# Clustered attention, feed-forward and soft mixture: narrowing in two slopes through PSUM, 128-column means, own PSUM tiles, low halves on VectorE, a new order

## The chip, the cores and the metric

The kernel runs on one core of one Trainium2 chip. The metric is device time in microseconds of one execution, the median over the timed runs; lower is better. Engines: PE (TensorE), with its weight loads shown apart as PEld, DVE (VectorE), ACT (ScalarE), POOL (GpSimd), SP (SyncE, which here only issues transfers).

## What is computed

Three stages over a batch of 2 with 8 heads, 768 positions and 64 columns a head; all data but w_in and w_out is float32.

```python
# attention, per batch and head; scale = 1/sqrt(64), 16 centroids per head
q_assign = argmax(q_n @ c_n.T); k_assign = argmax(k_n @ c_n.T)   # normalised rows
scores = where(q_assign[:, None] == k_assign[None, :], scale * q @ k.T, -1e9)
x = softmax(scores) @ v                       # -> x: 1536 tokens x 512
# feed-forward, w_in 512 x 2048, w_out 2048 x 512
h = x @ w_in; g = h * clip(h + 3, 0, 6) / 6; x = g @ w_out
# soft mixture: phi 512 x 32 slots, 8 experts of 4 slots, w1 512 x 1024, w2 1024 x 512
logits = x @ phi
slot_in = softmax(logits, over tokens).T @ x
slot_out[e] = relu(slot_in[e] @ w1[e]) @ w2[e]
out = softmax(logits, over slots) @ slot_out
```

w_in and w_out arrive as float64; the chip reads each number as two uint32 words and narrows it to float32.

## The kernel before

**Stages.** Heads 0 to 15 (head i is batch i // 8) go through attention. float32 products are made from float16 pairs (a high half and a low half) so that PE runs at its 16-bit rate. For each head: `cast_hi` and `cast_lo` make the halves of q and k (scaled by SQ = 64), transposed by DMA (head 0: by PE, in `turned`); `as_mm`, `as_max`, `as_put` find the cluster of each row; `cnt_mm` counts empty clusters and makes the mean of v with `wmean` (80 columns); `maxq`, `maxr`, `shift` find the row maxima (L531, L547, L556); then for six key blocks t `scores` (L569, L573), `exps` (L617 and a float16 high half through `high`, L342; or L610 where WHOLE names the block, which then stays float32), `plow` (the low half, by `low`, L352, on POOL) and `pv` (L639 to L660). `finish` divides (L672), `split_x` makes the halves of x.

**Weights.** w_in (8 blocks, `win`) and w_out (8 blocks, `wout`) are narrowed during the first heads by `narrow`: part 0 keeps the sign bits on DVE (L878) and scales the absolute value on ACT into PSUM (L880); part 1 shifts and joins on DVE inside PSUM (L883); part 2 joins the low word on DVE (L888). w_out goes back to DRAM as `wos`; `wphi1` to `wphi3` fold phi into w_out.

**Feed-forward.** 12 token blocks of 128: `hid` (L710), `act` (L727, L729, halves through L342 and L352, then the transpose of g: by DMA, or for the tiles in TURNED by PE into PSUM and copied out by ACT and DVE in turns, L751 and L753), `logits`, `colmax`, `dweights`, `dispatch`. The blocks of batch 0 run among the heads of batch 1; those of batch 1 after the last head.

**Experts.** `zsum` (L1193 on), `slot_in`, `slot_t`, `combine_weights`, `layer1`, `relu`, `turn`, `layer2`, `store2`, and for the last four experts column part by column part (PARTS) `layer2_part` (L1402), `slots_out`, `combine` with the output transfers. Their weights come in chunks (`fetch`, L1019 and L1041) into rooms: ring a (4 rooms, from the start), ring b (9, once attention's memory is given back in `close`), ring c (2, after `close2`), then tiles of earlier stages as they come free.

**Order.** Every function is a generator whose steps end in `yield`. ORDER is a list of event numbers; `flush` runs the next step of the named event, so the list fixes the order of the instructions on every engine and on SP's queue. ROOMS names the buffer of each tile. `keep` events are matmuls without use that keep PE running. Engines run their own queue in order; a step that waits holds what is behind it on its engine.

Of the kernel before, what the change touches and what calls it, by code (L numbers as in the profile page):

```python
# [1477 lines left out]
```

## Time and profile before

| what | us |
|---|---|
| median of 3 timed runs | 479.06 |
| lowest, highest | 476.38, 479.09 |
| span of the profiled execution | 475.5 |

The page gives no time for the profiled execution other than its span; the median of the timed runs is 3.6 us above it.

| engine | busy us | share of the span |
|---|---|---|
| PE | 437.2 | 92% |
| ACT | 316.9 | 67% |
| DVE | 284.3 | 60% |
| POOL | 251.1 | 53% |

Busy time is the time in which an engine had at least one instruction running. PE's matmuls overlap, and their ends are modelled. The share is a mean over stages with different limits, so the rows below are cut by stage.

### The profile page before, as it was taken

The numbers are of one execution on the slowest core, as the hardware profiler recorded it, in microseconds if no ns is written. First come the engines' busy times: TensorE is split into PE (matmuls) and PEld (weight loads), VectorE is DVE, ScalarE is ACT, GpSimd is POOL, SyncE is SP. The second block draws the span as 40 slices with busy tenths as digits, with TensorE's granted clock in tenths as the row PEclk, the third lists the DMA queues.
The fourth block names the chain that finished last, engine by engine and source line by source line (L and its number), as shares of the span: only waits on it lengthen the run. The fifth ranks groups of instructions, "written<-read, shape, count | busy, mean of one in ns | idle before, by whom it ended". The sixth has DMA issues, their size and how long they took to land.

```text
span 475.5 us, 11894 instructions
## 1 busy us (share of the span) xinstructions
PE 437.2 (92%) x4938; PEld 283.1 (60%) x4938; DVE 284.3 (60%) x497; ACT 316.9 (67%) x518; POOL 251.1 (53%) x227
## 2 busy tenths in 40 slices
PE   6779999999979999999999998989998999789973
PEld 5557678777767656656666666754545545442443
DVE  4899999998968387466667759513233223540222
ACT  7369899898965978876789998963545335600121
POOL 5326588785644555666698897984313233130000
PEclk9789999999999999999999999999999999999998
DMA  8777866946794689689473555005996799999998
GB/s 280 187 150 187 193 172 174 271 122 196 244 253 113 177 203 195 139 157 226 112 145 72 54 102 139 3 1 106 314 307 207 158 274 373 406 341 384 339 284 272
DMA packets 133813, 95.50 MB, mean 201 GB/s; under 512 B 96384, under 2 KB 119424, under 8 KB 133760
## 3 DMA queue, kind: packets, MB, share of 16 engines
q1 hardware_dynamic: 129088, 88.95, 71.2%
q10 hardware_dynamic: 4672, 5.80, 3.4%
q8 instruction: 38, 0.62, 0.5%
q14 instruction: 15, 0.12, 0.1%
HBM read 64.06 MB, written 7.34 MB: 150 GB/s over the span
## 4 chain that ended last, share of the span: by engine, by line
PE 66%; DVE 14%; ACT 8%; DMA 6%; issue 3%; POOL 2%; SPq 0%; ACTq 0%; DVEq 0%; POOLq 0%
PE h L710 26%; DVE mxs L547 4%; PE st L569 4%; PE sm L531 4%; PE st L573 4%; PE e L1345 3%; DMA wod<-in_moe_w_out_dram 3%; PE acc L639 2%; PE acc L652 2%; PE z L819 2%; DMA wk<-in_moe_w_dram 2%; ACT p L617 2%; PE acc L645 2%; PE acc L644 2%; PE o L1382 2%
## 5 line engine op out<-in xcount | busy, mean ns | idle before, releaser
L352 POOL TENSOR_TENSOR pp<-p,pp 128x768 f16<-128x768 f32 x72 | 119.7, 1667 | 56.1 <-ACT pp L342 28.0
L710 PE MATMUL h<-wq,xt 128*128 128x512 f16 x576 | 132.1, 379 | 0.0
L547 DVE TENSOR_REDUCE mxs<-sm 128x1 f32<-128x768 f32 x96 | 89.5, 952 | 15.7 <-PE sm L531 15.0
L710 PEld LDWEIGHTS <-xt 128*128 128x128 f16 x576 | 55.2, 98 | 62.0 <-issue 2.5
L352 POOL TENSOR_TENSOR ghl<-r,ghl 128x1024 f16<-128x1024 f32 (+1 forms) x25 | 50.4, 2017 | 61.1 <-ACT ghl L342 55.9
L617 ACT ACTIVATE p<-st 128x768 f32<-128x768 f32 x72 | 57.9, 805 | 15.2 <-PE st L573 13.7
L342 ACT ACTIVATE pp<-p 128x768 f16<-128x768 f32 x72 | 60.3, 842 | 1.4 <-PE acc L652 0.2
L569 PE MATMUL st<-qk1t 128*128 128x384 f16 x192 | 47.6, 329 | 5.5 <-ACT p L617 4.9
L531 PE MATMUL sm<-qk2t 80*128 80x384 f16 x192 | 45.9, 331 | 2.7 <-DVE mxs L547 0.9
L729 DVE SCALAR_TENSOR_TENSOR r<-r,h 128x1024 f32<-128x1024 f32 (+1 forms) x26 | 29.5, 1135 | 31.4 <-ACT r L727 31.3
L573 PE MATMUL st<-qk2t 102*128 102x384 f16 x192 | 47.5, 329 | 0.0
L727 ACT ACTIVATE r<-h,b_relu 128x1024 f32<-128x1024 f32 (+1 forms) x26 | 27.2, 1045 | 24.7 <-PE h L710 13.8
L645 PE MATMUL acc<-v,pp 128*128 128x64 f16 x432 | 36.1, 194 | 0.0
L644 PE MATMUL acc<-v,pp 128*128 128x65 f16 x432 | 36.1, 192 | 0.0
L352 POOL TENSOR_TENSOR qk<-qk,qk 128x768 f16<-128x768 f32 x15 | 24.7, 1645 | 21.7 <-ACT qk L342 20.5
L639 PE MATMUL acc<-v,pp 128*128 128x65 f32 x288 | 35.8, 274 | 0.3 <-DVE wp L973 0.2
L639 PEld LDWEIGHTS acc<-v,pp 128*128 128x128 f32 x288 | 34.6, 192 | 1.5 <-DVE mv L518 0.3
L342 ACT ACTIVATE ghl<-r 128x1024 f16<-128x1024 f32 (+1 forms) x26 | 25.7, 989 | 14.3 <-DVE r L729 10.5
L644 PEld LDWEIGHTS <-pp 128*128 128x128 f16 x432 | 31.2, 99 | 2.5 <-ACT pp L342 0.2
L645 PEld LDWEIGHTS <-pp 128*128 128x128 f16 x432 | 29.2, 96 | 2.1
L342 ACT ACTIVATE qk<-qk 128x768 f32<-128x768 f32 (+2 forms) x32 | 26.2, 817 | 1.8 <-DMA qk<-in_k_dram 0.9
L361 PE MATMUL kw<-ident,ident 128*128 128x256 f16 x136 | 23.4, 306 | 4.0 <-POOL ident L311 1.8
...
## 6 DMA issues: line engine op xcount, KB each, us to landing
...
```

Of the source, the lines that this page charges most:

```text
L342: nc.scalar.activation(out, in_, AF.Copy, scale=scale)
L352: (nc.vector if e == "v" else nc.gpsimd).tensor_tensor(out=out, in0=in_, in1=hi, op=ALU.subtract)
L531: nc.tensor.matmul(s[:, j, 0:384], d["qk2t"][0:80, n, 0], d["qk2t"][0:80, 3 * j : 3 * j + 3, 1], start=True, stop=True,)
L547: nc.vector.tensor_reduce(out=mxs[i % 2][:, 96 + n : 97 + n], in_=s[:, :, 0:384], op=ALU.max, axis=AX.XY)
L569: nc.tensor.matmul(s[:, j, 0:384], d["qk1t"][:, t, 1], d["qk1t"][:, 3 * j : 3 * j + 3, 0], start=True, stop=False)
L573: nc.tensor.matmul(s[:, j, 0:384], d["qk2t"][0 : 96 + NT, t, 1], d["qk2t"][0 : 96 + NT, 3 * j : 3 * j + 3, 0], start=False, stop=True,)
L617: nc.scalar.activation(p32, s[:, :, 0:384], AF.Exp, scale=sc_exp)
L639: nc.tensor.matmul(o, p32[:, j, r * P : (r + 1) * P], d["v32"][:, t], start=(t == 0 and n == 0), stop=False)
L644: nc.tensor.matmul(o, hi, v1[:, t, 0:65], start=(t == 0 and n == 0), stop=False)
L645: nc.tensor.matmul(o[:, 0:64], hi, v1[:, t, 65:129], start=False, stop=False)
L710: nc.tensor.matmul(s[:, fb % 2], xt[:, lhs], wq[fb][:, hl, kk], start=(n == 0), stop=(n == 11))
L729: nc.vector.scalar_tensor_tensor(out=g, in0=r, scalar=6.0 * SG, in1=sf, op0=ALU.min, op1=ALU.mult)
```

## The change

- `narrow`: part 0 shifts the low word right (DVE) and scales the high word on ACT with Prelu, whose slope for negative numbers is 2^32 times that for positive ones, so that the sign arrives at its bit with the shift; part 1 is gone; part 2 is one DVE pass that shifts the PSUM word left and joins the low word.
- `cast_hi` and `cast_lo`, heads 1 to 15: one ACT cast with the scale in it, in place of a scaling in place and a cast; the low half in two DVE instructions (q, k) with the scale, in place of one POOL subtraction. `castv_hi`: for heads 0 to 7 the float16 copy of v on POOL, not ACT.
- LATE, five softmax steps of heads 13 to 15: high and low half on DVE, not ACT and POOL.
- `cnt_mm`: counts and means with 128 weight columns, not 80; the one-hot rows live in two tiles of their own (`ohs`).
- `turned`: q and k in a PSUM tile each. `act`: the turned tile is copied out by one DVE instruction for both blocks (its branch to ACT is never taken, since `last` comes only with an odd first block). `layer1`: a PSUM tile for each half. `combine_weights`: `cT` copied by one DVE instruction.
- Ring b has ten rooms, ring c one. PARTS is (384, 128), not (256, 128, 128); the w2 of the last four experts is fetched in other pieces; `combine` writes the output of part 0 in two transfers per batch.
- ORDER and ROOMS are new in full: 2701 entries, before 2722.

```diff
 ORDER = (
...
+LATE = {(13, 4), (14, 1), (14, 4), (15, 1), (15, 4)}
-NRB = 9
-NRC = 2
+NRB = 10
+NRC = 1
...
-    wmean = cp.tile([P, 80], F16, name="wmean")
+    wmean = cp.tile([P, P], F16, name="wmean")
...
-            high("a", d["qk"], d["qk"], SQ)
-            yield
-            high("a", hi, x)
+            high("a", hi, x, SQ)
...
-        if i:
-            low("p", lo, x, hi)
-        else:
-            for a in range(2):
-                low("v", lo[:, :, a], x[:, :, a], hi[:, :, a], SQ)
+        for a in range(2):
+            low("v", lo[:, :, a], x[:, :, a], hi[:, :, a], SQ)
+            if i == 0:
                 yield
...
-        high("a", v1s[i % NV][:, :, 0:64], f[:, :, 0:64])
+        (nc.gpsimd.tensor_copy if i < H else nc.scalar.copy)(v1s[i % NV][:, :, 0:64], f[:, :, 0:64])
...
-            k5 = oh.rearrange("p a n c -> p (a n) c")[:, NT + n - 4 : NT + n + 1].rearrange("p n c -> p (n c)")
-            nc.tensor.matmul(pm[0:80, 400:401], k5, ones, start=(n == 0), stop=(n == NT - 1))
+            k8 = oh[:, NT + n - 4 : NT + n + 4].rearrange("p n c -> p (n c)")
+            nc.tensor.matmul(pm[:, 400:401], k8, ones, start=(n == 0), stop=(n == NT - 1))
...
-        high("a", ph, p32)
+        if (i, t) in LATE:
+            nc.vector.tensor_copy(ph, p32)
+        else:
+            nc.scalar.copy(ph, p32)
...
-            low("p", pl, p32, ph)
+            low("v" if (i, t) in LATE else "p", pl, p32, ph)
...
-        for f in range(f1 - f0):
-            if (f0 + f) % 2:
-                nc.vector.tensor_copy(d["gt"][:, f0 + f], tp[:, f])
-            else:
-                nc.scalar.copy(d["gt"][:, f0 + f], tp[:, f])
-            yield
+        if last and f0 % 2 == 0:
+            nc.scalar.copy(d["gt"][:, f0:f1], tp)
+        else:
+            nc.vector.tensor_copy(d["gt"][:, f0:f1], tp)
+        yield
...
-            nc.vector.tensor_scalar(out=s, in0=hi, scalar1=0x80000000, scalar2=None, op0=ALU.bitwise_and)
+            nc.vector.tensor_scalar(out=s, in0=lo, scalar1=29, scalar2=None, op0=ALU.logical_shift_right)
             yield
-            nc.scalar.activation(t.bitcast(F32), hi.bitcast(F32), AF.Abs, scale=2.0**-111)
-        elif part == 1:
-            t = raw[nm, "t"]
+            nc.scalar.activation(t, hi.bitcast(F32), AF.Prelu, scale=2.0**-111, alpha=2.0**32)
+        elif part == 2:
             nc.vector.scalar_tensor_tensor(
-                out=t, in0=t, scalar=3, in1=raw.pop((nm, "s")), op0=ALU.logical_shift_left, op1=ALU.bitwise_or
-            )
-        else:
-            t = raw.pop((nm, "t"))
-            nc.vector.scalar_tensor_tensor(
-                out=dst.bitcast(U32), in0=lo, scalar=29, in1=t, op0=ALU.logical_shift_right, op1=ALU.bitwise_or
+                out=dst.bitcast(U32),
+                in0=raw.pop((nm, "t")).bitcast(U32),
+                scalar=3,
+                in1=raw.pop((nm, "s")),
+                op0=ALU.logical_shift_left,
+                op1=ALU.bitwise_or,
             )
...
-    PARTS = [(0, 256), (256, 128), (384, 128)]
+    PARTS = [(0, 384), (384, 128)]
...
+            for j in range(4):
+                src = w2[e + j].rearrange("(p c) d -> p c d", c=8)
+                nc.sync.dma_start(ts[j][0], src[:, 5:8, 0:384])
+                yield
+            for lo, hi in ((1, 4), (4, 8)):
+                for j in range(4):
+                    src = w2[e + j].rearrange("(p c) d -> p c d", c=8)
+                    nc.sync.dma_start(ts[j][1][:, lo - 1 : hi - 1], src[:, lo:hi, 384:512])
+                    yield
+            return
+        if kind == "d":
...
+            nc.sync.dma_start(u, src[:, 1:5, 0:384])
+            yield
+            nc.sync.dma_start(t[:, 0:512], src[:, 0])
...
-        nc.vector.tensor_copy(cT[:, 0:NT], tp[:, 0:NT])
-        nc.scalar.copy(cT[:, NT:], tp[:, NT:])
+        nc.vector.tensor_copy(cT, tp)
...
-            sl["hp", g] = pss(f"e1_{g}")
+            sl["hp", g] = (pss(f"e1_{g}")[:, 0], psm(f"e1b_{g}"))
```

## Rows read from the trace of the kernel before

**Rows 1.** Busy time by leg; columns: us, busy us (instructions) of each engine, clock, DMA

```profile
0.00:154.30 154.30, 137.68 (x1562) 108.02 (x1566) 133.04 (x218) 123.16 (x188) 93.42 (x105) 0.96 0.73 196
154.30:319.50 165.20, 161.66 (x2034) 104.56 (x2027) 101.30 (x183) 138.87 (x224) 123.56 (x80) 1.00 0.62 124
319.50:416.30 96.80, 90.77 (x774) 47.27 (x771) 34.38 (x63) 46.85 (x90) 29.85 (x16) 1.00 0.87 264
416.30:475.50 59.20, 47.14 (x574) 23.23 (x574) 15.61 (x34) 8.06 (x16) 4.31 (x26) 0.97 1.00 324
```

**Rows 2.** Timeline of DVE, the divisions of heads 7 and 15: start us, us, what

```profile
154.31 0.56 DVE L672 TENSOR_TENSOR xa<-acc,den 128x384 f32<-128x384 f32 x1
...
319.51 0.56 DVE L672 TENSOR_TENSOR xa<-acc,den 128x384 f32<-128x384 f32 x1
```

**Rows 3.** Busy time from 300 us to the end of head 15, columns as above

```profile
300.00:319.50 19.50, 17.31 (x309) 13.16 (x307) 5.54 (x15) 15.98 (x20) 17.95 (x12) 1.00 0.01 2
```

**Rows 4.** The chain that ended last, from 400 us on: start us, us, what

```profile
410.67 1.91 ACT gt L753 x2
...
416.33 1.13 PE zt L1193 x8
...
450.29 8.33 DMA wk<-in_moe_w_dram
```

**Rows 5.** DVE's groups in leg 1: line, shapes, count, busy us, mean ns, idle before

```profile
L883 DVE SCALAR_TENSOR_TENSOR nt_i<-nt_i,nw_i 128x1024 uint32<-128x1024 uint32 x8 | 9.8, 1225 | 0.1
L888 DVE SCALAR_TENSOR_TENSOR wi<-wi,nt_i 128x1024 uint32<-128x1024 uint32 x8 | 9.8, 1222 | 0.2
...
L883 DVE SCALAR_TENSOR_TENSOR nt_o<-nt_o,nw_o 128x1024 uint32<-128x1024 uint32 x6 | 7.4, 1227 | 0.6 <-ACT nt_o L880 0.4
```

**Rows 6.** Groups of ACT by form, the whole span: table loads

```profile
L837 ACT ACT_TABLE_LOAD x1 | 1.3, 1283 | 1.2 <-PEq L1462 1.2
L306 ACT ACT_TABLE_LOAD x1 | 1.3, 1283 | 0.0
```

**Rows 7.** Groups by form, the whole span: DVE, then ACT, then POOL

```profile
L350 DVE SCALAR_TENSOR_TENSOR qk<-qk,qk 128x384 f16<-128x384 f32 x2 | 1.1, 558 | 4.0 <-ACT qk L342 4.0
...
L342 ACT ACTIVATE qk<-qk 128x768 f32<-128x768 f32 x15 | 12.5, 835 | 0.9 <-DMA qk<-in_k_dram 0.9
...
L342 ACT ACTIVATE v<-v 128x384 f16<-128x384 f32 x16 | 8.4, 526 | 0.1
...
L753 ACT COPY gt<-gp 128x1024 f16<-128x1024 f16 x8 | 7.8, 1005 | 0.0
...
L352 POOL TENSOR_TENSOR pp<-p,pp 128x768 f16<-128x768 f32 x72 | 119.7, 1667 | 56.1 <-ACT pp L342 28.0 <-issue 12.6 <-DVE nt_o L883 5.3
...
L352 POOL TENSOR_TENSOR qk<-qk,qk 128x768 f16<-128x768 f32 x15 | 24.7, 1645 | 21.7 <-ACT qk L342 20.5 <-POOL v L352 0.7 <-PE sm L554 0.5
...
L419 POOL COPY qk<-qk 128x768 f16<-128x768 f16 x1 | 1.2, 1211 | 1.1 <-ACT qk L342 1.1
```

**Rows 8.** Groups of PE's weight loads by form, the whole span

```profile
L644 PEld LDWEIGHTS <-pp 128*128 128x128 f16 x432 | 31.2, 99 | 2.5 <-ACT pp L342 0.2
...
L507 PEld LDWEIGHTS <-wmean 128*80 128x80 f16 x96 | 8.4, 127 | 0.0
```

**Rows 9.** Busy time in three windows of the tail, columns as above

```profile
404.00:416.00 12.00, 9.21 (x128) 5.86 (x126) 6.79 (x16) 7.45 (x19) 2.35 (x3) 1.00 1.02 407
446.00:454.00 8.00, 6.41 (x80) 2.58 (x82) 0.91 (x2) 0.55 (x1) 0.00 (x0) 1.00 1.15 317
456.00:464.00 8.00, 6.02 (x93) 4.31 (x91) 3.30 (x7) 3.14 (x6) 0.00 (x0) 1.00 1.01 284
```

**Rows 10.** L878 (duration min/median/max ns), then POOL's and DVE's timeline from 9.5 us

```profile
L878 DVE TENSOR_SCALAR nw_i<-wi x8: 681/685/1932, 10.2 to 119.3; 128x1024 uint32<-128x1024 uint32 x8
...
9.93 1.64 POOL L352 TENSOR_TENSOR qk<-qk,qk 128x768 f16<-128x768 f32 x1 [3.93 <-ACT qk L342]
...
10.18 1.93 DVE L878 TENSOR_SCALAR nw_i<-wi 128x1024 uint32<-128x1024 uint32 x1 [2.21 <-DMA wi<-in_moe_w_in_dram]
```

More of the change, by code (lines that the diff above doesn't have):

```diff
@@ L303, in clustered_attention_ffn_softmoe @@
     mvs = [ap.tile([P, 129], F16, name=f"mv_{i}", bufs=1) for i in range(3)]
+    ohs = [ap.tile([P, 16, C], F16, name=f"ohs_{i}", bufs=1) for i in range(2)]
     def second():
@@ L314, in consts @@
             nc.gpsimd.memset(rank[:, c : c + 1], float(C - c))
+        for t in ohs:
+            nc.gpsimd.memset(t[:, 12:16], 0.0)
         yield
@@ L383, in cast_hi @@
         hi, lo = halves(d["qk1"])
+        if i:
+            yield
         x = d["qk"].rearrange("p a n d -> p n a d")
         if i:
-            high("a", d["qk"], d["qk"], SQ)
-            yield
-            high("a", hi, x)
+            high("a", hi, x, SQ)
         else:
@@ L394, in turned @@
     def turned(out, in_, nm):
-        tp = pss(nm).rearrange("p a b -> p (a b)").bitcast(F16)[:, 0 : 12 * P]
-        tp = tp.rearrange("p (n a q) -> p n a q", a=2, q=P)
+        tp = []
         for a in range(2):
+            t = (psm(f"{nm}_1") if a else pss(f"{nm}_0")[:, 0]).bitcast(F16)[:, 0 : NT * P].rearrange("p (n q) -> p n q", q=P)
             for n in range(NT):
-                nc.tensor.transpose(tp[:, n, a], in_[:, n, a], ident16)
+                nc.tensor.transpose(t[:, n], in_[:, n, a], ident16)
+            tp.append(t)
             yield
         for a in range(2):
-            (nc.vector.tensor_copy if a else nc.scalar.copy)(out[:, :, a], tp[:, :, a])
+            (nc.vector.tensor_copy if a else nc.scalar.copy)(out[:, :, a], tp[a])
             yield
@@ L472, in as_max @@
         nc.vector.tensor_reduce(out=mx2, in_=sc, op=ALU.max, axis=AX.X)
-        oh = ap.tile([P, 2, NT, C], F16, tag="oh", name=f"oh_{i}")
+        oh = ohs[i % 2][:, 0:12].rearrange("p (a n) c -> p a n c", a=2)
         nc.vector.tensor_tensor(
@@ L499, in cnt_mm @@
         d = st[i]
-        oh = d["oh"]
+        oh = ohs[i % 2]
         v1 = v1s[i % NV]
@@ L503, in cnt_mm @@
         for n in range(NT):
-            k5 = oh.rearrange("p a n c -> p (a n) c")[:, NT + n - 4 : NT + n + 1].rearrange("p n c -> p (n c)")
-            nc.tensor.matmul(pm[0:80, 400:401], k5, ones, start=(n == 0), stop=(n == NT - 1))
+            k8 = oh[:, NT + n - 4 : NT + n + 4].rearrange("p n c -> p (n c)")
+            nc.tensor.matmul(pm[:, 400:401], k8, ones, start=(n == 0), stop=(n == NT - 1))
         for n in range(NT):
-            nc.tensor.matmul(pm[0:80, 0:65], wmean, v1[:, n, 0:65], start=(n == 0), stop=False)
-            nc.tensor.matmul(pm[0:80, 0:64], wmean, v1[:, n, 65:129], start=False, stop=(n == NT - 1))
+            nc.tensor.matmul(pm[:, 0:65], wmean, v1[:, n, 0:65], start=(n == 0), stop=False)
+            nc.tensor.matmul(pm[:, 0:64], wmean, v1[:, n, 65:129], start=False, stop=(n == NT - 1))
         yield
@@ L838, in centroids @@
         yield
-        sq = ap.tile([P, D], F32, tag="oh", name="csq")
+        sq = ap.tile([P, D], F32, tag="csq", name="csq", bufs=1)
         ss = sm.tile([P, 1], F32, tag="tm", name="css")
@@ L850, in centroids @@
         nc.vector.reciprocal(r, y)
-        cn = ap.tile([P, D], F32, tag="oh", name="cn")
+        cn = ap.tile([P, D], F32, tag="cn", name="cn", bufs=1)
         nc.vector.tensor_scalar(out=cn, in0=c32, scalar1=r, scalar2=SQ, op0=ALU.mult, op1=ALU.mult)
@@ L904, in win @@
     def win(fb, kp, part):
+        if part == 1:
+            return
         t = raw["i", fb, kp]
@@ L926, in wout @@
     def wout(j, hf, part):
+        if part == 1:
+            return
         t = raw["o", j, hf]
@@ L985, in clustered_attention_ffn_softmoe @@
     rooms = ["a"] * NRA + ["b"] * NRB + ["c"] * NRC + ["x.g", "w0", "w1", "w2", "w3", "x.r", "ghl", "gt", "ghl"]
-    rooms += ["a"] * 2 + ["b"] * 8 + ["c"] * 2
+    rooms += ["a"] * 2 + ["b"] * 9 + ["c"]
     wt_ = {}
+    wd = {}
     ring = {"n": 0}
@@ L1007, in fetch @@
             for j in range(4):
-                t = room(n + j, rooms[n + j], 2048, f"wk_{n + j}").rearrange("p (a c d) -> p a c d", a=2, c=8)
-                ts.append(t)
-                for a in range(2):
-                    wt_[kind, e + j, 1 + a] = (t[:, a, 0:4], t[:, a, 4:8])
-            for p, (c0, w) in enumerate(PARTS):
-                if p:
-                    np = 2 if p == 2 else 1
-                    for c in range(np):
-                        cc = slice(8 // np * c, 8 // np * (c + 1))
-                        for j in range(4):
-                            src = w2[e + j].rearrange("(p c) d -> p c d", c=8)
-                            nc.sync.dma_start(ts[j][:, p - 1, cc], src[:, cc, c0 : c0 + w])
-                            yield
+                t = room(n + j, rooms[n + j], 2048, f"wk_{n + j}")
+                u = t[:, 0:1152].rearrange("p (c d) -> p c d", c=3)
+                v = t[:, 1152:2048].rearrange("p (c d) -> p c d", c=7)
+                for c in range(1, 8):
+                    wd[e + j, 1, c] = v[:, c - 1]
+                for c in range(5, 8):
+                    wd[e + j, 0, c] = u[:, c - 5]
+                ts.append((u, v))
+            for j in range(4):
[7 more added lines that the diff above has]
+                    yield
+            return
+        if kind == "d":
+            src = w2[e].rearrange("(p c) d -> p c d", c=8)
+            t = room(n, rooms[n], 2048, f"wk_{n}")
+            u = t[:, 512:2048].rearrange("p (c d) -> p c d", c=4)
+            wd[e, 0, 0] = t[:, 0:384]
+            wd[e, 1, 0] = t[:, 384:512]
+            for c in range(1, 5):
+                wd[e, 0, c] = u[:, c - 1]
+            nc.sync.dma_start(u, src[:, 1:5, 0:384])
+            yield
+            nc.sync.dma_start(t[:, 0:512], src[:, 0])
+            yield
             return
@@ L1315, in combine @@
         c0, w = PARTS[p]
-        nt = 512 // w if w > 128 else 3
-        nu = NT // nt
-        k, a = (("w2", 0), ("w3", 0), ("gt", 0), ("gt", 2), ("w1", 2), ("b0", 0))[2 * p + b]
-        ob = lt2k(k, a, [NT, w], F32)
-        ps = []
-        for u in range(nu):
-            po = pss(f"po_{p}_{b}_{u}")[:, 0] if (nu * b + u) % 4 > 1 else psm(f"po_{p}_{b}_{u}")
-            po = po[:, 0 : nt * w].rearrange("p (n d) -> p n d", n=nt)
+        dst = out[b * S : (b + 1) * S].rearrange("(p n) d -> p n d", n=NT)
+        dma = (nc.sync if b else nc.scalar).dma_start
+        if p == 0:
+            four = lt2k(("w2", "w3")[b], 0, [4, w], F32)
+            two = lt2k("gt", 2 * b, [2, w], F32)
+        else:
+            four = lt2k(("w1", "b0")[b], 2 - 2 * b, [NT, w], F32)
+        nt = 2 if p == 0 else 3
+        ps = []
+        for u in range(NT // nt):
+            if p == 0:
+                po = pss(f"po_{p}_{b}_{u}")[:, :, 0:w]
+            else:
+                po = pss(f"po_{p}_{b}_{u}")[:, 0] if b else psm(f"po_{p}_{b}_{u}")
+                po = po[:, 0 : nt * w].rearrange("p (n d) -> p n d", n=nt)
             for j in range(nt):
@@ L1329, in combine @@
         for u, po in enumerate(ps):
-            o = ob[:, u * nt : (u + 1) * nt]
-            if (nu * b + u) % 2:
+            o = two if p == 0 and u == 2 else four[:, u * nt : (u + 1) * nt]
+            if (u + b) % 2:
                 nc.vector.tensor_scalar(out=o, in0=po, scalar1=1.0 / (SO * SC), scalar2=None, op0=ALU.mult)
@@ L1335, in combine @@
             yield
-        (nc.sync if b else nc.scalar).dma_start(
-            out=out[b * S : (b + 1) * S].rearrange("(p n) d -> p n d", n=NT)[:, :, c0 : c0 + w], in_=ob
-        )
+            if p == 0 and u == 1:
+                dma(out=dst[:, 0:4, c0 : c0 + w], in_=four)
+                yield
+        if p == 0:
+            dma(out=dst[:, 4:NT, c0 : c0 + w], in_=two)
+        else:
+            dma(out=dst[:, :, c0 : c0 + w], in_=four)
     def layer1(g, kk):
         if kk == 0:
-            sl["hp", g] = pss(f"e1_{g}")
+            sl["hp", g] = (pss(f"e1_{g}")[:, 0], psm(f"e1b_{g}"))
         for f in range(2):
@@ L1345, in layer1 @@
                 nc.tensor.matmul(
-                    sl["hp", g][32 * j : 32 * j + 32, f],
+                    sl["hp", g][f][32 * j : 32 * j + 32],
                     sl["sts"][:, kk],
@@ L1356, in relu @@
         for f in range(2):
-            src = sl["hp", g][:, f].rearrange("p (a c) -> p c a", c=8)
+            src = sl["hp", g][f].rearrange("p (a c) -> p c a", c=8)
             if f:
@@ L1404, in layer2_part @@
                     hw(NG - 1, c, j),
-                    wv("d", E - 4 + j, p, c)[:, 0:w],
+                    wd[E - 4 + j, p, c],
                     start=(c == 0),
```

4 lines of the change are left out of this document (1 added, 3 removed), and 345 rows, old and new, of tables (ORDER, ROOMS).

## The prediction

> **What bounds the kernel now.** I first read the busy time by stage, cut at three instructions [rows 1, 2]: the start of the last VectorE division of batch 0 (head 7, 154.31 us), that of head 15 (319.51 us) and the first matmul of `zsum` (416.33 us, in [rows 4]). That makes four legs of 154.3, 165.2, 96.8 and 59.2 us. The reader is to see a different limit in each. In leg 1 no engine is idle: DVE 133.0, PE 137.7, ACT 123.2 of 154.3 us, so a saving on one alone is soon met by the next. Leg 2 is PE's: 161.7 of 165.2. Its end is thinner on PE: from 300 us to the end of head 15 POOL is busy 17.95 and ACT 15.98 of 19.5 us, DVE 5.54, DMA 0.01 [rows 3]. Leg 3 is PE's too (90.8 of 96.8). In leg 4 the DMA engines are busy all the time (share 1.00), and the chain of waits shows PE stopped for weights: 8.33 us from 450.29 us to the `layer2_part` matmuls, till 458.62 [rows 4].
>
> The profiled execution has a span of 475.5 us. The median of the timed runs is 479.06, so 3.6 us lie around the span; I make the sum on the span and add 3.6.
>
> **The change, part by part.** The durations are those of the named rows; how many instructions fall in a leg is counted from the two order strings, cut at the same three steps.
>
> *Narrowing.* Each of the 16 blocks loses one VectorE pass (L883). In leg 1 there are 8 and 6 of them at 1.225 and 1.227 us [rows 5]: 17.2 us of DVE work gone; 2 more (2.5 us) go in leg 2. What stays costs the same: the first pass is still one scalar operation on 1024 strided words (L878), the last still reads one operand from PSUM and one from SBUF (as L888, 1.222 us). Prelu for Abs on ACT is one pass of the same 1024 elements with an immediate scale, so I exclude a gain; above, it costs a table load each way, 1.283 us [rows 6], if the function is not in the loaded table. I take no change; the load is a rival.
>
> *Low halves of q and k.* For heads 1 to 15, ACT's in-place scaling (0.835 us) and POOL's subtraction (1.645 us) go [rows 7]; DVE gets two scaled subtractions of 384 elements. Head 0 already runs that form: 0.558 us each [rows 7], so 1.116 a head. After's order has ten such heads in leg 1: 11.2 us, and five in leg 2: 5.6.
>
> *Net of leg 1.* DVE loses 17.2 and gains 11.2: -6.0. ACT loses 9 scalings (7.5 us) and 8 copies of v (0.526 each, 4.2 us), which POOL takes. POOL's price for such a copy is bounded by its 768-element copy, 1.211 us, and by nothing; half of 1.211 is nearest, 0.6 each, 4.8 us, covered by the 9 x 1.645 = 14.8 us that leave POOL. So DVE is lightened least and still ends last: I take 6.0 off the leg. Bounds: nothing (PE, at 137.7 us, may have needed the time anyway) and 16.6 us, where PE would be busy without a gap.
>
> *Late heads.* Five softmax steps of heads 13 to 15 move cast and low half to DVE. POOL loses 5 x 1.667 = 8.3 us [rows 7], ACT five casts. Each of DVE's ten new instructions has 768 elements; I bound it by the 0.558 us of 384 elements and twice that. So 5.6 to 11.2 us, in a stretch where DVE is busy 5.54 of 19.5: covered. Leg 2 has only 165.2 - 161.7 = 3.5 us in which PE does nothing; what PE loses between matmuls inside its busy time can't be read. I take 3.0; bounds nothing and 6 (POOL's stretch after 300 us shorter by most of its 8.3).
>
> *128-column means.* Weights of 80 columns load in 0.127 us, of 128 columns in 0.099 [rows 8]: 288 x 0.028 = 8.1 us of load time, from nothing to all of it on PE's path. Loads overlap matmuls; I take it as part of leg 2's 3.0. The rule of the Trainium skill that fits (TensorE: Matmul & The Clock Gate, section Weight-path perf modes) says that a fast weight load needs exactly 128 weights of a type other than FP32; the trace agrees, 0.099 against 0.127 us, and by the rule alone the whole 8.1 us would come off, in place of leg 2's 3.0: 460.5.
>
> *Own PSUM tiles, evictions.* Before, ACT and DVE copy the halves of `gt` one after the other, and at 410.67 us two ACT copies (1.91 us) are on the chain [rows 4]. After, DVE alone copies, and ACT loses 8 x 1.005 = 8.0 us [rows 7]. All but the last token's copies lie under PE's matmuls, and cost PE time only if that cover is gone. I take 1.0 off leg 3, half of the 1.91; bounds nothing and 1.9. The two `e1` tiles and the single `cT` copy are costed at nothing: they lie in leg 4 under the weights' transfer; without that cover they would be worth under 1 us.
>
> *Tail.* The last four experts' w2 (8.4 MB) is fetched in other pieces. Before: half in 1 KB rows, half in 512 B rows. After: 1.05 MB in 2 KB, 5.5 MB in 1.5 KB, 1.84 MB in 512 B rows. The trace moves 407 GB/s with large rows, 317 while the 1 KB rows are in flight, 284 with 512 B rows [rows 9]. Before: 4.19/0.317 + 4.19/0.284 = 28.0 us. After: 2.6 + 15.2 (1.5 KB rows halfway, 0.362) + 6.5 = 24.3; with the bounds for the 1.5 KB rows 22.6 to 26.5. I take 3.5 off leg 4; bounds nothing and the 8.3 us of the wait. That ring b gets a tenth room and c loses one changes no byte: nothing. SP's queue is reordered, the transposes of x for tokens 8 to 11 ahead of most fetches; SP has no compute behind it, so that costs only if the transfers stand idle for it, which leg 4's share of 1.00 would then show as less.
>
> *New wait.* On DVE the low halves wait for ACT's cast. Behind them in DVE's queue stand the row maxima that free PSUM for PE's next score matmuls. Head 0 shows such a wait of 4.0 us [rows 7].
>
> **Sum.** 475.5 - 6.0 - 3.0 - 1.0 - 3.5 = 462.0; with 3.6 us: 465.6, say 465.5.
>
> **The rivals.**
> 1. *DVE and POOL collide.* At 10.18 us DVE's L878 took 1.93 us against a median of 0.685, and ended 0.54 us after the POOL subtraction (9.93 to 11.57) that it overlapped [rows 10]: it stood still until POOL was done. If the new DVE subtractions behave so, each pair in leg 1 loses up to 1.25 us, ten pairs 12.5; half of that takes back leg 1's 6 us: 471.5. For it: POOL is busy 93 of 154 us [rows 1]. Against: the 15 POOL subtractions that left. The Trainium skill (SBUF — State Buffer, section Who interferes with whom) states that a DVE instruction with two SBUF inputs contends with a POOL instruction that reads SBUF, as well as one in a two-port mode; the row above shows the latter only. By that rule this rival would be the forecast.
> 2. *PE needs its time.* PE holds 137.7 and 161.7 us of legs 1 and 2; if its work sets both, only legs 3 and 4 gain: 474.6.
> 3. *More of it comes.* Leg 1 gives 12 (ACT and DVE relieved together), leg 2 its 6, leg 4 its 8.3: 452.
> 4. *Slower: DVE waits for ACT.* Ten heads in leg 1, up to the 4.0 us of head 0 each. It decides above 13.5/10 = 1.35 us a head; at 2.5 a head 490. Against it: ACT's part of the chain is one pass shorter.
> 5. *Slower: Prelu is not in Exp's table.* 28 loads of 1.283 us in leg 1 are 35.9 us of ACT; ACT has 123.2 - 11.7 + 35.9 = 147.4 us, more than DVE's 127, and at DVE's present share of the leg (0.86) the leg takes 171: 488. Against it: Abs, Relu and Copy run among the Exps with only the two loads of the start [rows 6].
>
> **How the numbers follow.** Forecast 0.58, rival 1 0.13, 2 0.11, 3 0.09, 4 0.05, 5 0.04. About 1% is what a measurement of this kernel can tell from no change, 474.3 to 483.9. Faster: the forecast, rival 3 and most of rival 1, 0.78; same: rival 2 and the rest of 1, 0.13; slower 0.09. The range runs from rival 3 to rival 2, 453 to 475; it leaves out the two slower ones and the far sides of 2 and 3. The forecast's own range is 459 to 471.
>
> **What would show it.** L883's group is gone and DVE's busy time in leg 1 is some 6 us less; the L350 group has 32 instructions near 0.56 us (rival 1: a mean well above it, or POOL's subtractions stretched); the division of head 7 starts near 148, that of head 15 near 310, `zsum` near 406; two table loads in all (rival 5: 34); the wait for the last weights under 5 us. The forecast is wrong if head 7 ends no earlier than now, or if leg 4 is longer than 59 us.

## The result: slower by 1.1%, and the loss is in leg 1

The changed kernel takes 482.77 us (median; the kernel before beside it 477.35). The ratio is 1.0112, 95% interval 1.0085 to 1.014: slower by more than can be taken for no change, where 465.5 us was forecast. The profiled execution has a span of 481.2 us against 475.5 before and 462.0 in the sum. Here and below a time is the median of all timed runs and a ratio is of fast runs alone (those within 1.5% of their kernel's fastest), so the two can differ by a little.

First the busy time by leg, as in [rows 1], cut at the same three steps (division of head 7 at 163.81 us, of head 15 at 329.87, first matmul of `zsum` at 421.79). Columns: us, busy us (instructions) of PE, PEld, DVE, ACT, POOL, the granted clock as a share of full speed, DMA share, GB/s.

```profile
0.00:163.80 163.80, 143.78 (x1572) 109.72 (x1573) 138.91 (x225) 117.05 (x178) 84.59 (x107) 0.94 0.75 192
163.80:329.90 166.10, 161.38 (x2018) 103.41 (x2017) 115.69 (x198) 125.49 (x201) 106.92 (x68) 1.00 0.59 122
329.90:421.80 91.90, 90.22 (x799) 48.09 (x795) 39.43 (x67) 40.73 (x87) 29.85 (x16) 1.00 0.92 270
421.80:481.20 59.40, 45.76 (x480) 19.38 (x480) 15.40 (x30) 6.95 (x15) 4.05 (x26) 0.95 0.92 318
```

| leg | before | forecast | after | after less forecast |
|---|---|---|---|---|
| 1 | 154.3 | 148.3 | 163.8 | +15.5 |
| 2 | 165.2 | 162.2 | 166.1 | +3.9 |
| 3 | 96.8 | 95.8 | 91.9 | -3.9 |
| 4 | 59.2 | 55.7 | 59.4 | +3.7 |

Leg 1 carries the result. VectorE was to fall there from 133.0 to 127 us and rose to 138.9. Its groups in leg 1, the answer to [rows 5] and to the L350 row of [rows 7] (line, shapes, count, busy us, mean ns, idle before):

```profile
L353 DVE SCALAR_TENSOR_TENSOR qk<-qk,qk 128x384 f16<-128x384 f32 x22 | 18.3, 871 | 0.1
L886 DVE SCALAR_TENSOR_TENSOR wi<-nt_i,nw_i 128x1024 uint32<-128x1024 uint32 x8 | 9.7, 1216 | 0.1
L882 DVE TENSOR_SCALAR nw_i<-wi 128x1024 uint32<-128x1024 uint32 x8 | 8.3, 1039 | 0.5 <-DMA wi<-in_moe_w_in_dram 0.4
...
L882 DVE TENSOR_SCALAR nw_o<-wod 128x1024 uint32<-128x1024 uint32 x6 | 6.3, 1044 | 2.8 <-DMA wod<-in_moe_w_out_dram 2.7
```

The third pass of the narrowing (L883 before) is gone and the last one (L886) costs what it did. The low halves (L353) average 0.871 us, not 0.558, and the first pass of the narrowing (L882) 1.04, not 0.84 and 0.69. Over the whole span the 32 low halves are 545 ns at the least, 551 in the median and 2485 at the most: most are as forecast, a few are very long. What a long one looks like, in the timeline of POOL and DVE (start us, us, what):

```profile
89.92 1.64 POOL L355 TENSOR_TENSOR pp<-p,pp 128x768 f16<-128x768 f32 x1 [2.02 <-ACT pp L624]
...
91.32 3.07 DVE L353 SCALAR_TENSOR_TENSOR qk<-qk,qk 128x384 f16<-128x384 f32 x2
91.53 2.44 POOL L355 TENSOR_TENSOR wq<-wi,wq 128x1024 f16<-128x1024 f32 x1
```

The pair of head 7 takes 3.07 us where 1.02 is a pair's time beside no subtraction of POOL. It ends at 94.39, 0.42 us after POOL's subtraction (93.97). Every pair above 1.03 us (eight of sixteen) and every L882 above 0.8 us (ten of sixteen) overlaps a POOL instruction, and where that one can be told apart in the timeline it ends 0.4 to 0.9 us after it. POOL is hardly held up in turn: its 67 subtractions of `pp` average 1.677 us, before 1.667. That is the standing still of [rows 10], met again and again.

What it does to PE is in the chain of waits (start us, us, what) and in the busy time of the 3 us stretches behind it, columns as above:

```profile
91.32 3.07 DVE qk L353 x2
...
95.98 0.86 DVE mxs L549
```

```profile
93.00:96.00 3.00, 2.83 (x32) 2.31 (x30) 2.87 (x6) 1.92 (x3) 2.17 (x2) 1.00 0.10 21
96.00:99.00 3.00, 1.27 (x13) 0.97 (x13) 2.97 (x5) 1.48 (x4) 0.22 (x1) 1.00 0.58 111
99.00:102.00 3.00, 3.00 (x32) 2.59 (x32) 3.00 (x4) 2.33 (x4) 3.00 (x3) 0.61 1.14 117
102.00:105.00 3.00, 3.00 (x41) 2.02 (x39) 2.90 (x5) 2.28 (x3) 1.58 (x3) 0.82 1.05 388
```

The row maxima (`mxs`), which free PSUM for PE's next scores, queue behind the pair and come late. PE is busy 1.27 of the 3 us from 96 on. Then the granted clock falls to 0.61, so for most of the next 3 us TensorE runs at 1.2 GHz in place of 2.4. Between 24 and 164 us the clock falls five times, at 45, 79, 100, 113 and 144 us, each time when PE had not been busy throughout (1.27 of 3 us in the row above). Not all five are the standing still's: f2 below, in which no low half stands still, has falls at 47 and 135 us. The 1572 matmuls of leg 1 took 143.8 us here; in the kernel below whose clock stays at 1.00 (h2) they took 133.1.

### The profile page after: what moved, and what is told of

Same layout as the page of the kernel before. It is cut to its first block, busy times and chain, and to the rows that moved or that the text cites. A ratio compares the mean times of both kernels' runs of the same rounds, so it can differ in the third digit from the quotient of the medians.

```text
span 481.2 us, 11686 instructions
## 1 busy us (share of the span) xinstructions
PE 441.2 (92%) x4858; PEld 280.6 (58%) x4858; DVE 309.4 (64%) x519; ACT 290.2 (60%) x478; POOL 225.4 (47%) x217
## 4 chain that ended last, share of the span: by engine, by line
PE 60%; DVE 17%; DMA 10%; ACT 5%; issue 3%; POOL 1%; SPq 1%; ACTq 0%; DVEq 0%; POOLq 0%
PE h L715 22%; PE sm L533 5%; PE st L571 4%; DVE mxs L549 4%; DMA wk<-in_moe_w_dram 4%; PE st L575 4%; DMA qk2t<-qk 3%; PE acc L644 2%; DVE qk L353 2%; PE acc L650 2%; PE acc L657 2%; PE acc L649 2%; PE z L823 2%; PE kw L364 2%; PE tp L955 2%
## 5 line engine op out<-in xcount | busy, mean ns | idle before, releaser
L355 POOL TENSOR_TENSOR pp<-p,pp 128x768 f16<-128x768 f32 x67 | 111.9, 1677 | 79.5 <-ACT pp L624 52.2
L624 ACT CAST pp<-p 128x768 f16<-128x768 f32 x67 | 55.2, 831 | 0.9
L571 PE MATMUL st<-qk1t 128*128 128x384 f16 x192 | 49.1, 338 | 3.5 <-DVE wi L886 1.2
L575 PE MATMUL st<-qk2t 102*128 102x384 f16 x192 | 49.0, 337 | 1.0 <-DVE qk2t L558 1.0
L732 ACT ACTIVATE r<-h,b_relu 128x1024 f32<-128x1024 f32 (+1 forms) x26 | 27.2, 1048 | 26.5 <-PE h L715 18.3
L644 PEld LDWEIGHTS acc<-v,pp 128*128 128x128 f32 x288 | 36.6, 200 | 1.8 <-DVE mv L520 0.7
L644 PE MATMUL acc<-v,pp 128*128 128x65 f32 x288 | 37.4, 282 | 0.2 <-DVE mv L520 0.2
L649 PEld LDWEIGHTS <-pp 128*128 128x128 f16 x432 | 31.9, 100 | 3.3 <-DVE pp L622 0.5
L650 PEld LDWEIGHTS <-pp 128*128 128x128 f16 x432 | 29.5, 97 | 2.7 <-issue 0.2
L355 POOL TENSOR_TENSOR xhl<-xa,xhl 128x384 f16<-128x384 f32 x16 | 15.8, 991 | 29.2 <-ACT xhl L345 27.6
L575 PEld LDWEIGHTS <-qk2t 102*128 102x128 f16 x192 | 19.3, 101 | 15.3 <-issue 3.7
L533 PEld LDWEIGHTS <-qk2t 80*128 80x128 f16 x192 | 17.0, 101 | 17.5 <-issue 7.0
```

Of the source, the lines that this page charges most:

```text
L355: (nc.vector if e == "v" else nc.gpsimd).tensor_tensor(out=out, in0=in_, in1=hi, op=ALU.subtract)
L533: nc.tensor.matmul(s[:, j, 0:384], d["qk2t"][0:80, n, 0], d["qk2t"][0:80, 3 * j : 3 * j + 3, 1], start=True, stop=True,)
L571: nc.tensor.matmul(s[:, j, 0:384], d["qk1t"][:, t, 1], d["qk1t"][:, 3 * j : 3 * j + 3, 0], start=True, stop=False)
L575: nc.tensor.matmul(s[:, j, 0:384], d["qk2t"][0 : 96 + NT, t, 1], d["qk2t"][0 : 96 + NT, 3 * j : 3 * j + 3, 0], start=False, stop=True,)
L624: nc.scalar.copy(ph, p32)
L644: nc.tensor.matmul(o, p32[:, j, r * P : (r + 1) * P], d["v32"][:, t], start=(t == 0 and n == 0), stop=False)
```

## The experiments

Two theories stood against each other. C (collision): VectorE's new instructions stand still while POOL works, and that is the loss. O (order): the parts do what was forecast, and the new order loses the time. A third, L (load), came with them: the plain work put on VectorE is too much. Ratios are to the kernel before, run beside each, with 95% intervals. The changed kernel's own is 1.0112 (1.0085 to 1.014).

| kernel | time, us | ratio | legs 1, 2, 3, 4 of its profile |
|---|---|---|---|
| e1 before + narrowing | 471.33 | 0.9869 (0.9836 to 0.9902) | not read |
| e2 before + low halves | 519.38 | 1.0869 (1.0822 to 1.0916) | not read |
| e3 before + both | 504.57 | 1.0585 (1.0543 to 1.0627) | not read |
| e4 after, low halves on POOL | 471.77 | 0.9878 (0.9831 to 0.9924) | 151.9, 169.0, 92.6, 58.8 |
| f1 e4 + plain load on VectorE | 475.07 | 0.9955 (0.992 to 0.9991) | 153.4, 167.5, 92.4, 59.4 |
| f2 after, one-input form | 476.39 | 0.994 (0.9905 to 0.9976) | 154.8, 164.6, 91.9, 58.9 |
| f3 after, no late heads | 492.09 | 1.0324 (1.0299 to 1.0349) | 164.0, 174.4, 92.0, 59.5 |
| f4 after, 80 columns | 482.66 | 1.0139 (1.0114 to 1.0164) | 158.8, 166.7, 91.9, 59.5 |
| g1 after, 7 heads on POOL | 471.42 | 0.9863 (0.982 to 0.9907) | 149.3, 165.9, 92.2, 59.2 |
| g2 e1 + late heads | 478.31 | 1.0023 (1.0002 to 1.0045) | 148.3, 172.3, 96.9, 60.4 |
| g3 after, gt copies shared | 490.01 | 1.0224 (1.0174 to 1.0274) | 159.2, 165.8, 98.2, 59.0 |
| g4 after, v copies on ACT | 482.73 | 1.0107 (1.0066 to 1.0149) | 166.2, 165.8, 91.9, 59.5 |
| h1 e1 + gt copies on VectorE | 472.39 | 0.9849 (0.9792 to 0.9906) | 147.4, 165.5, 96.5, 62.3 |
| h2 after, 5 heads on POOL | 472.23 | 0.9844 (0.979 to 0.9897) | 147.7, 166.1, 92.0, 59.1 |
| h3 e3, one-input form | 499.44 | 1.0519 (1.0455 to 1.0583) | 164.7, 170.3, 97.0, 59.6 |

The profiled executions of e1, e2 and e3 took 506.1, 523.8 and 512.2 us, more than any other run of each, so their legs are not compared. One profile's leg 1 is not exact: in the five kernels that keep the low halves of the changed kernel (after, f3, f4, g3, g4) it lies between 158.8 and 166.2 us. On the whole it is longest where the mean granted clock of the leg is lowest: 158.8 at 0.98 (f4), 159.2 at 0.97 (g3), 164.0 at 0.95 (f3), 163.8 at 0.94 (after), 166.2 at 0.92 (g4). No kernel without the long pairs of leg 1 and in this order is above 154.8.

**e1, e2, e3: single parts in the old order.**

```diff
 narrow:   # e1, e3: two-slope form, the second of three steps empty
-  s = hi & 0x80000000;  t = Abs(hi);  t = t << 3 | s;  dst = lo >> 29 | t
+  s = lo >> 29;  t = Prelu(hi);  dst = t << 3 | s
 cast_hi / cast_lo:   # e2, e3: heads 1 to 15
-  ACT x *= SQ;  ACT hi = x;  POOL lo = x - hi
+  ACT hi = x * SQ;  DVE lo = x * SQ - hi, twice 384 elements
```

e1 

> The kernel before, in its own order, with only the two-slope narrowing (14 VectorE passes of 1.23 us fewer in leg 1, the low halves stay on POOL). Theory C, that VectorE's new instructions stand still while POOL subtracts: VectorE's busy time up to head 7's division falls by 17 us less some 2 to 4 us of stretched first passes, and with VectorE the fullest engine of leg 1 the time falls by 4 to 9 us against before. Theory O, that the new parts do what was forecast and the new order loses the time: the same fall, 4 to 9 us, but then the two changes together (next but one) fall too. Theory P, that PE needs leg 1's time anyway: within 2 us of before.

e2 

> The kernel before, in its own order, with only the low halves of q and k of heads 1 to 15 on VectorE in one scaled step. Theory C: the mean of the 32 subtractions is 0.8 to 0.95 us and not 0.56, VectorE's leg 1 grows by 15 to 18 us and the time is 6 to 14 us longer than before. Theory O: the mean stays near 0.56 us, VectorE grows by 11 us, ACT and POOL are relieved by 7.5 and 15 us, and the time is 0 to 5 us longer.

e3 

> The kernel before, in its own order, with the narrowing and the low halves together. Theory C: 17 us off VectorE and 17 to 21 us on it again, so 477 to 485 us, like the changed kernel, though the order is the old one. Theory O: 468 to 473 us, since the order is the old one and the parts do what was forecast.

The narrowing alone gains 1.3%, as C and O said; P falls. The low halves alone lose 8.7%, three times what C allowed and far above O's 5 us, although their mean in e2's trace, 0.81 us, lies where C had put it. With the narrowing the loss is 5.9%, far more than the changed kernel's 1.1% and outside both ranges. So in the old order something costs more than both theories hold; h3 below takes that up.

**e4: the low halves back on POOL, in the new order.**

```diff
 cast_hi (i > 0):
-  high("a", hi, x, SQ)
+  high("a", d["qk"], d["qk"], SQ); high("a", hi, x)
 cast_lo (i > 0):
-  low("v", lo[:, :, a], x[:, :, a], hi[:, :, a], SQ)   # a = 0, 1
+  low("p", lo, x, hi)
```

> The changed kernel in its own order with the low halves of heads 1 to 15 put back on POOL (ACT scales in place and then casts, in one step). Theory C: VectorE's leg 1 loses 17 us, POOL gains 16 and ACT 7.5, and the time is 4 to 10 us shorter than the changed kernel's, 473 to 479. Theory O: the order is what costs, so the time stays within 3 us of the changed kernel's 482.8 or grows, as ACT and POOL get work that the order has no room for.

471.77 us: 11 us less than the changed kernel and a little under C's range, by this one edit and with the new order kept. O falls as the reason of leg 1's loss. C or L is left.

**f1, f2: the load without the standing still.**

```diff
 f1 (e4, and beside low("p", ...)):
+  nc.vector.tensor_reduce(out=junk, in_=x[:, :, a], op=ALU.max, axis=AX.XY)   # a = 0, 1
 f2 (the changed kernel):
-  low("v", lo[:, :, a], x[:, :, a], hi[:, :, a], SQ)
+  nc.vector.tensor_scalar(out=lo[:, :, a], in0=x[:, :, a], scalar1=2.0**-4, scalar2=0.0, ..., accum_out=junk)
```

f1 

> The changed kernel with the low halves of heads 1 to 15 on POOL again, and beside each of them two VectorE reductions of 384 elements (one SBUF input, result unused) at the place in VectorE's queue where its two subtractions stood: VectorE's load without the subtraction. Theory L, that VectorE's plain load of 1.1 us a head is what costs: 479 to 483 us, as the changed kernel. Theory C, that most of the loss is the standing still behind POOL and the lateness it brings: the reductions take 0.4 to 0.6 us each with no stretched ones among them, and the time is 472 to 477.

f2 

> The changed kernel, but the two subtractions of heads 1 to 15 are replaced on VectorE by a multiplication of the same 384 elements with one SBUF input that also gives its sum (the low half is then not the low half: the subtraction is left out). Theory C: no instance is stretched, the mean is 0.4 to 0.6 us where the changed kernel had 0.88, and the time is 471 to 477 us. Theory L: the durations fall the same, and the time stays at 479 to 483.

Neither form is ever long. The row of f1's reductions and then of f2's multiplications (least, median, most ns):

```profile
L418 DVE TENSOR_REDUCE junk<-qk x30: 541/543/555, 11.8 to 255.2; 128x1 f32<-128x384 f32 x30
```

```profile
L416 DVE TENSOR_SCALAR_CACHE_REDUCE qk<-qk x30: 540/547/554, 12.3 to 254.2; 128x384 f16<-128x384 f32 x30
```

They do meet POOL: 12 of f1's 30 reductions and 10 of f2's 30 multiplications run wholly inside a subtraction of POOL. In f1's timeline a pair of reductions runs beside a subtraction, the second of them wholly inside it, and neither engine's work is longer for it:

```profile
86.77 1.64 POOL L355 TENSOR_TENSOR qk<-qk,qk 128x768 f16<-128x768 f32 x1 [3.08 <-ACT qk L345]
...
86.74 1.01 DVE L418 TENSOR_REDUCE junk<-qk 128x1 f32<-128x384 f32 x2
```

Leg 1 of f2, columns as above:

```profile
0.00:154.78 154.78, 138.13 (x1572) 106.83 (x1573) 132.14 (x245) 116.68 (x178) 83.60 (x107) 0.97 0.79 203
```

f2 has the changed kernel's order and the load that was forecast for it, at 0.546 us an instruction, and 0.08 us more to read each sum. It no longer reads ACT's cast, but VectorE had waited for that only 0.1 us in leg 1, so this is not the difference. It is 1.7% faster than the changed kernel (0.994 against 1.0112), some 8 us (6 by the medians), and leg 1 of its profile is 9.0 us shorter. Part of the 9.0 is the clock: against g3, which has the changed kernel's leg 1 and the same mean clock there as f2 (0.97), it is 4.4 us. f1 says what the plain load costs over e4: 0.8%, some 4 us, with intervals that just touch. So C holds for the larger part, L for a smaller one. By the Trainium skill (SBUF — State Buffer, section Who interferes with whom) a reduction never contends with POOL on trn2 and a scaled subtraction with two SBUF inputs does; f1's 541 to 555 ns and the 2485 ns above agree.

**g1, h2: POOL only for the heads that stood still.**

```diff
 cast_hi, cast_lo:
+  if i in (4, 5, 6, 7, 8, 11, 12):   # g1; h2: (4, 5, 6, 7, 8)
+      as in e4
   else: as in the changed kernel
```

g1 

> The changed kernel with the low halves on POOL only for heads 4 to 8, 11 and 12, the seven whose subtractions stood still in the profile of the changed kernel; the other eight stay on VectorE. Theory C: the stretched instances are mostly gone, and the time is that of the kernel with all of them on POOL or better, 468 to 475 us. Rival, that POOL's work meets whatever is left on VectorE: other instances are stretched now and the time lies between, 475 to 481.

h2 

> The changed kernel with the low halves on POOL for heads 4 to 8 only, so heads 11 and 12 stand still on VectorE again. Leg 2 is PE's (161 of 166 us busy): theory C with PE's cover gives the time of the kernel with seven heads on POOL within 1 us, 470 to 473; if standing still costs there as it does in leg 1, 1.5 to 4 us more.

Legs 1 to 3 of h2, and its 3 us stretches at the times at which the changed kernel's clock fell (the work in them is not the same, since h2 is ahead); columns as above:

```profile
0.00:147.69 147.69, 133.12 (x1572) 103.80 (x1573) 126.15 (x216) 120.07 (x183) 92.03 (x112) 1.00 0.83 213
147.69:313.82 166.13, 161.69 (x2017) 103.38 (x2015) 116.60 (x198) 125.44 (x201) 106.91 (x68) 1.00 0.57 122
313.82:405.86 92.04, 90.24 (x799) 48.09 (x795) 39.46 (x67) 40.72 (x87) 29.84 (x16) 1.00 0.91 270
...
96.00:99.00 3.00, 2.64 (x29) 1.99 (x28) 2.97 (x3) 2.04 (x4) 3.00 (x3) 1.00 0.02 5
99.00:102.00 3.00, 3.00 (x40) 2.60 (x38) 2.83 (x8) 2.79 (x5) 2.92 (x3) 1.00 1.14 91
```

Five pairs of heads 1 to 10 stay on VectorE in leg 1, each 1.01 to 1.03 us, and leg 1 falls to 147.7 us. VectorE is busy 126.2 us in it. The forecast had 127 in 148. PE stays busy (2.64 of 3 us from 96 on) and its clock is 1.00 in the whole leg. g1, which has the same leg 1, took 149.3 us there, so 1.6 us between two profiles mean nothing. Both kernels beat both given ones: 471.4 and 472.2 us, 1.4 and 1.6% faster than before. But e1 (0.9869), e4 (0.9878) and h1 (0.9849) have intervals that overlap with theirs: nothing in this study is shown to be faster than the narrowing alone in the old order. In h2 heads 11 and 12 stand still again:

```profile
L353 DVE SCALAR_TENSOR_TENSOR qk<-qk,qk x22: 546/551/2505, 6.8 to 248.3; 128x384 f16<-128x384 f32 x22
```

Their two pairs (3.33 and 2.97 us) lie in leg 2, whose length is that of g1 within 0.2 us (166.1 against 165.9). Head 14's pair, the shortest of the eight long ones, is 1.31 us in both. So standing still costs where VectorE feeds PE without slack, and nothing that shows where PE covers it.

**h3: the old order without the standing still.**

```diff
 e3, with f2's multiplication in place of the subtraction
```

> The kernel before, in its own order, with the narrowing and with the two one-input multiplications of 384 elements on VectorE in the place of the low halves of heads 1 to 15 (the subtraction is left out, as in f2_low_one_input). If VectorE's standing still is what made the narrowing with the low halves 28 us slower than before in this order, the time is near before's, 474 to 482 us. If it is the place in VectorE's queue, which the old order chose for a POOL instruction, the low halves come late all the same: 490 to 503 us, with PE waiting over 5 us for the transposed q and k in the first 130 us.

Still 5.2% slower than before, against 5.9% with the subtractions, with intervals that overlap. So in the old order the standing still is at most a small part of it. The largest wait of PE in the first 130 us (total us, times, longest):

```profile
PE as L447 <- DMA qk1t<-qk: 10.1, 2, 5.9
```

The kernel before has no such wait; e3, with the subtractions, has 11.9 us of it. How the longer of the two comes about, in the timelines of ACT, VectorE and PE:

```profile
73.69 0.84 ACT L342 ACTIVATE qk<-qk 128x768 f16<-128x768 f32 x1 [0.29 <-DVE mxs L549]
...
83.16 0.55 DVE L411 TENSOR_SCALAR_CACHE_REDUCE qk<-qk 128x384 f16<-128x384 f32 x1
...
89.48 0.50 PE L447 MATMUL as<-ct,qk1t 128*128 128x32 f16 x12 [5.91 <-DMA qk1t<-qk]
```

The old order put `cast_lo` where POOL had time. On VectorE it starts 8.6 us after ACT's cast is done, behind other work in the queue; the transposing DMA starts late, and PE waits. These waits are 10.1 us of a loss of some 24; the rest is not traced. So the new low halves need another order than the old one, and the new order is not what loses.

**f3, g2: late heads.**

```diff
 f3 (after):  -LATE = {(13, 4), (14, 1), (14, 4), (15, 1), (15, 4)}   +LATE = set()
 g2 (e1):     +LATE as in the changed kernel, in exps and plow
```

f3 

> The changed kernel with the five late softmax steps of heads 13 to 15 back on ACT and POOL. By the prediction they give leg 2 part of its 3.0 us, so without them 1 to 3 us longer than the changed kernel, all of it between the divisions of heads 12 and 15. Rival: PE's matmuls bound that stretch anyway, within 1 us.

g2 

> The kernel before, in its own order, with the narrowing and with the five late softmax steps of heads 13 to 15 on VectorE. If POOL bounds the end of batch 0 (17.95 of 19.5 us busy from 300 us on), the stretch from head 12's division to head 15's is 3 to 8 us shorter than before's 38.6 us, and the time is 464 to 469 us. Rival, that PE bounds it: the time of the narrowing alone, 470 to 472.

Leg 2 of f3, then of g2:

```profile
163.96:338.31 174.35, 164.91 (x2014) 105.18 (x2013) 106.81 (x188) 128.94 (x206) 113.69 (x73) 0.98 0.55 116
```

```profile
148.34:320.62 172.28, 164.68 (x2034) 106.03 (x2027) 108.79 (x191) 134.76 (x219) 115.36 (x75) 0.98 0.58 119
```

Both expectations miss, also in the stretch that they name, from head 12's division to head 15's: 44.0 us in f3 against 35.5 in the changed kernel, 45.6 in g2 against 38.6 before. Taken out of the new order, the five steps cost 8.3 us of leg 2 (174.4 against 166.1). Put into the old one, they cost 6.8 (172.3 against h1's 165.5). An order made with the steps on one engine loses by having them on another, either way round. What the edit itself is worth is not separated by these runs.

**g3, h1: the copies of gt.**

```diff
 act (g3, after):
-  nc.vector.tensor_copy(d["gt"][:, f0:f1], tp)
+  for f in range(f1 - f0): (DVE if (f0 + f) % 2 else ACT) copies d["gt"][:, f0 + f]
 act (h1, e1): the reverse
```

g3 

> The changed kernel with the copies of gt shared by ACT and VectorE again. By the prediction 1 us longer (bounds 0 and 1.9); if these copies are what made leg 3 4.9 us shorter, 3 to 5 us longer, with leg 3 above 95 us.

h1 

> The kernel before, in its own order, with the narrowing and with the whole copy of gt on VectorE. If the copies themselves are what made leg 3 shorter, leg 3 is 3 to 6 us shorter than before's 96.8, leg 1 some 6 us shorter by the narrowing, and the time is 464 to 468 us, the best of all. If leg 3's gain belongs to the new order, leg 3 stays within 1.5 us of 96.8 and the time is that of the narrowing alone, 470 to 473.

Leg 3 of g3, then legs 1 and 3 of h1:

```profile
324.98:423.21 98.23, 90.80 (x800) 48.17 (x796) 35.86 (x65) 48.09 (x95) 29.87 (x16) 1.00 0.86 254
```

```profile
0.00:147.37 147.37, 134.39 (x1562) 106.05 (x1566) 119.39 (x204) 122.66 (x188) 92.80 (x105) 0.98 0.78 205
...
312.87:409.38 96.51, 91.00 (x775) 47.35 (x772) 38.47 (x65) 40.10 (x82) 29.85 (x16) 0.99 0.87 264
```

In the new order the edit carries leg 3: undone, 98.2 against 91.9 us. In the old order it gives 0.3 (96.5 against 96.8). So leg 3's gain needs both the edit and the order. h1 also shows the narrowing in a profile: leg 1 of 147.4, 6.9 below before.

**f4, g4: two small parts.**

```diff
 f4: -wmean = cp.tile([P, P], ...)   +wmean = cp.tile([P, 80], ...)   # and 80 columns of one-hots
 g4: -(nc.gpsimd.tensor_copy if i < H else nc.scalar.copy)(v1s ...)   +nc.scalar.copy(v1s ...)
```

f4 

> The changed kernel with weights of 80 columns again in the means and counts. If the load time is on PE's path, up to 8 us longer than the changed kernel (288 loads by 0.026 us); if loads lie under the matmuls, within 1 us, and the load rows say 0.127 us again.

g4 

> The changed kernel with the copies of v of heads 0 to 7 back on ACT. By the prediction ACT and POOL have room either way: within 1 us. Theory C gives a small gain, since eight POOL instructions of 0.6 us fewer can be in VectorE's way: 0 to 3 us shorter.

Weight loads of `wmean`, first of the changed kernel, then of f4 (us, mean ns):

```profile
L510 PEld LDWEIGHTS <-wmean 128*128 128x128 f16 x96 | 7.1, 101 | 0.0
```

```profile
L509 PEld LDWEIGHTS <-wmean 128*80 128x80 f16 x96 | 8.4, 127 | 0.0
```

The loads are shorter as costed and the time is the same: 1.0139 with 80 columns, 1.0112 with 128, intervals overlapping. The rule of the Trainium skill (TensorE: Matmul & The Clock Gate, section Weight-path perf modes) holds for the load, 0.101 against 0.127 us; but the time does not follow, so the saved load time was not on PE's path here. The copies of v change nothing either (1.0107).

## Why the prediction was wrong, by its own steps

**What bounds the kernel.** Both signs of being wrong that the prediction named came: head 7 ends later (163.8 us, before 154.3), and leg 4 is longer than 59 us (59.4). The reading of leg 1 held in part: VectorE's busy time is on the way to PE's next scores. In the kernel before and those of the new order leg 1 rises with it: 126.2 us gives 147.7 (h2), 125.7 gives 149.3 (g1), 130.9 gives 153.4 (f1), 132.1 gives 154.8 (f2), 133.0 gives 154.3 (before), 138.9 to 139.7 give 158.8 to 166.2 (after, f3, f4, g3, g4). Under some 126 us less of it brings no more: h1 with 119.4 has 147.4, and e4 with 121.6 and POOL at 101 us has 151.9. VectorE's busy time is not all: h3, with 128.6 us of it and PE's waits for the DMA, has 164.7.

**The 3.6 us around the span** were mis-sized. In every run whose span is on record the time lies 1.7 to 2.2 us above the span; the 3.6 set a median against the span of another execution.

**Narrowing.** The 14 passes left as said, and the gain stands alone (e1, h1). "What stays costs the same" failed: the first pass went from 10.8 to 14.6 us in leg 1, since more of its instances stood still (12.9 in h1, whose low halves stay on POOL). Prelu took no table load; the two rows of ACT's table loads are those of before [rows 6].

**Low halves: the step that failed.** The term was 11.2 us, ten heads by 1.116. It measured 6.0 more: 18.3 us for the 22 instructions of eleven heads (head 0 among them) where 0.558 each gives 12.3. With the first pass that is 9.8 us, most of the 11.9 by which VectorE missed the forecast of leg 1. The price was taken from head 0, whose pair ran while POOL had no subtraction, and moved to places where POOL is busy 93 of 154 us [rows 1]. The one row that showed the other price [rows 10] was made a rival and not the term.

**Rival 1** was the mechanism. Its price in VectorE's time, half of ten pairs by 1.25 us, was 6.2, and 6.0 came over the forecast's price: five of the ten pairs were long, by 0.5 to 2.1 us. What it left out is what follows from that: late row maxima, PE's gaps and then the lower clock. Without the standing still of the low halves leg 1 is 9.0 us shorter (f2, 4.4 at an equal clock). With that it took back more than the 6.0 us forecast for the leg, and legs 2 and 4 missed by 3.9 and 3.7 us besides, so the time passed the 471.5 us given for this rival. That the gaps bring the clock down is read from the traces; no run changed the clock alone. f2's leg 1 is still 6.5 us over the forecast's 148.3: its first pass takes 15.2 us, reading the sums some 1.6, and its clock is 0.97. The argument against the rival, that 15 subtractions leave POOL, did not look at when the others run: in leg 1 POOL is still busy 84.6 of 163.8 us. The rule of the Trainium skill that stood beside this rival (SBUF — State Buffer, section Who interferes with whom) agrees with the trace: a pair with two SBUF inputs took 3.07 us beside POOL's subtraction and 1.02 without one.

**New wait.** VectorE's wait for ACT's cast did not come: 0.1 us idle in front of the 22 low halves, against 4.0 for head 0 before [rows 7]. Rival 4 named the wrong wait. In the old order there is one, and it is PE's, for the transposing DMA behind a late VectorE (h3, in which VectorE does not read the cast at all).

**Leg 2.** -3.0 was forecast, +0.9 came. PE was busy 161.7 us before and 161.4 after, so only its 3.5 us of gaps could go; the loads that the term counts in were worth nothing (f4: 166.7 with 80 columns, 166.1 with 128). The low halves that stood still there cost nothing that shows (h2). The stretch of the late heads did become 3.1 us shorter (35.5 against 38.6 us), but the new order also moves work across its start, and the rest of the leg grew by 4.0. The late heads are bound to the order, and their part stays open.

**Leg 3.** -1.0 was forecast, -4.9 came. "All but the last token's copies lie under PE's matmuls" was wrong: PE's gaps in leg 3 went from 6.0 us (96.8 less 90.8) to 1.7, and with the copies shared again they are 7.4 (g3). In the old order the edit leaves them at 5.5 (h1), so why the new one profits stays open.

**Leg 4.** -3.5 was forecast, +0.2 came. The chain of waits of the changed kernel (start us, us, what):

```profile
452.61 9.02 DMA wk<-in_moe_w_dram
461.63 0.04 issue
461.67 2.12 PE o L1435 x18
```

The last weights end 39.8 us after `zsum` starts, before 42.3 [rows 4]: 2.5 us won. But behind them 19.6 us are left, before 16.9. The first part of the output grew from 256 to 384 columns. Before, its slot outputs (`so`) were multiplied at 455.99 us, ahead of the last weights (458.62); now at 463.73, behind them (461.63). The first store of the output starts 6.75 us behind the last weights, before 3.8. The wait for the last weights is 9.02 us, where under 5 was to show the step right. The sum counted the transfer and not what follows it. By how much the larger rows and by how much the new order of fetches moved the last weights is not separated. This is read from the two traces; the tail was not changed alone.
